# One plan for the order of all engines' instructions in the expert units

## The chip, the cores and the metric

The kernel runs on one core of a Trainium2 chip. The metric is device time in microseconds, the median of three runs; lower is better. Engines are named as in the profile: PE is TensorE (PEld its weight loads), DVE is VectorE, ACT is ScalarE, POOL is GpSimd, SP is SyncE, which here only issues DMAs.

## What is computed

Three stages follow one another: attention with pooled queries, a mixture of eight experts with one expert for each token, and a feed-forward block with g = h cos h. `w_in` and `w_out` of the last stage come as 64-bit floats.

```python
def _attn_ref(q, k, v):                      # (4, 8, 1152, 64)
    q_pool = q.reshape(B, H, S // 2, 2, D).mean(axis=3)
    scores = scale * np.matmul(q_pool, k.transpose(0, 1, 3, 2))
    attn = np.exp(scores - np.max(scores, axis=-1, keepdims=True))
    attn = attn / (np.sum(attn, axis=-1, keepdims=True) + 1e-09)
    return np.matmul(attn, v).astype(np.float32)

def _moe_ref(x, w_gate, w1, w2):             # 2304 tokens, 512 wide, 8 experts, 1024 hidden
    logits = x @ w_gate
    expert_idx = np.argmax(logits, axis=1)
    ...
    for e in range(E):
        mask = expert_idx == e
        h = np.maximum(x[mask] @ w1[e], 0.0)
        out[mask] = gate_w[mask, None] * (h @ w2[e])

def _moe2_ref(x, w_in, w_out):               # 512 -> 2048 -> 512
    h = x @ w_in
    g = h * np.cos(h)
    return (g @ w_out).astype(np.float32)
```

## The kernel before

**Stages.** Attention runs over 32 heads in an order that a `Plan` lays down (steps with times, sorted and traced in that order; `Plan.tie` then ties TensorE's instructions, and only those, to this order). Routing counts the tokens of each expert and writes each token's number to a slot table in HBM. The experts follow, then the cosine blocks of 512 tokens.

**Precision.** Each float32 operand is split into a high and a low part, so a product is three matmuls (high x high, high x low, low x high). Making a high part is a copy on ScalarE, a low part a subtraction on VectorE or GpSimd.

**Expert units.** The experts are sorted by size and handled in twelve units (`UNIT`, L473): ten of 256 tokens, the last two of 128. Units 0 to 2 belong to the first expert, 3 and 4 to the second, 5 and 6 to the third, 7 to 11 to one expert each. A unit (`Experts.unit`, L960) works through four chunks of the hidden width. For a full unit, `first` makes 24 matmuls into a `ph` bank (two banks), ScalarE makes `hh` with a Relu, VectorE `hl`; `second` makes 24 matmuls of 512 columns with `hh` and `hl` into two `py` banks. First products run two chunks ahead (`HP = 2`). A half unit has the tokens as stationary operand: `tokens_first`, a Relu copy `hs` on ScalarE, two transposes by TensorE (`turned`), then `hh`, `hl` and `second`. At a unit's end `py` is scaled by the gate to `ys`, the token's number is copied beside it, and ScalarE's queue stores it to `y_d`.

**Work around the units.** (1) Gathers: `Tokens` loads 128 slot numbers `ix` and fetches the token rows `xg` by an indirect DMA on GpSimd, TensorE transposes them, `xh` and `xl` are made (`split_transposed`, L1171), and one column of `xg`, the gate, is copied by VectorE (L1089). (2) Weights: a chunk's `w1` and `w2` are loaded by SP into one of three `raw` buffers, ScalarE makes the high half, VectorE or GpSimd (`PLOW`: chunk 3) the low half (`weight_steps`, L1119; `Pipe`, L1149). An expert has eight such halves; they go into the buffers of the expert two before it. (3) Narrowing (`Narrow.step`, L1208): 32 steps turn the 64-bit words of `w_in` and `w_out` into float32: a load on SP, five instructions on VectorE, two on ScalarE, one multiply on GpSimd (L1229), and a store. `NSTEP` (L509) says how many each unit gets. (4) The first cosine block's rows are gathered and transposed (`load_block`, L1092).

**What sets the order.** The framework traces all instructions in the order of the Python code and then schedules them, engine by engine, with a timeline of its own; an instruction runs in the queue of its engine in the order so found, and waits on semaphores. `issue_after(x)` ties a block's instructions behind `x` on `x`'s engine. In the experts, only such ties stand: weight loads, narrowing steps and gathers are traced between the chunks of a unit:

```python
            for k in range(NSTEP[u]):
                between[k * NCH // NSTEP[u]].append((1, step))
```

## Time and profile before

| | us |
|---|---|
| median of three runs (lowest to highest) | 1257.46 (1253.23 to 1261.61) |
| the profiled execution | 1258.61 |
| its span, from the first to the last instruction | 1257.0 |
| attention, up to unit 0's first matmul | 543.7 |
| unit 0 | 24.5 |
| units 1 to 11 | 270.1 |
| cosine blocks | 418.7 |

Over the span TensorE is busy 94%, VectorE 74%, ScalarE 58%, GpSimd 44%. The busy time of matmuls is modelled, and matmuls overlap; the pace is read from their starts. An engine handles its queue in order, so an instruction that waits holds all behind it. A bracket such as [5.23 <-DVE hl_u L987] gives the idle time of the engine before the instruction and what ended it. A row of a stretch gives its bounds, its length, the busy time and count of each engine's instructions, the granted clock of TensorE as a share of full speed, the mean busy share of the 16 DMA engines, and what they moved. In rows 2 the first stretch holds units 1 to 11; the others are units 1, 2, 3 to 7, 8, 9, 10 and 11.

### The profile page before, as it was taken

Reading aid. Unit: us, or ns where it says so; the run is one execution under the profiler, and the core shown is the slowest. Engines: PE = TensorE matmul, PEld = TensorE weight load, DVE = VectorE, ACT = ScalarE, POOL = GpSimd, SP = SyncE. Lnnn points to the kernel's source line nnn. Section 1 sums busy time; section 2 is a strip of 40 time slices with the busy share of each in tenths; the row PEclk is TensorE's granted clock in tenths of the full one; section 3 lists DMA queues with packets and bytes.
Section 4 is the critical chain, followed back from the end, with each engine's and each line's share of the span. In section 5 each row is a group of like instructions: output and inputs, shape, how many; then the busy total and the mean of one; then the engine's idle time right before and its main releaser. Section 6 shows DMA issues by size and latency. Waiting matters only on the chain. (4 is left out here: it accounts for less than half of the span.)

```text
span 1257.0 us, 26782 instructions
## 1 busy us (share of the span) xinstructions
...
## 2 busy tenths in 40 slices
...
GB/s 198 116 104 137 138 148 116 111 113 142 124 118 96 101 41 118 58 106 118 234 287 300 270 292 288 281 171 123 18 48 24 1 30 40 1 51 1 1 34 17
DMA packets 116729, 148.20 MB, mean 118 GB/s; under 512 B 32336, under 2 KB 73072, under 8 KB 116592
## 3 DMA queue, kind: packets, MB, share of 16 engines
...
q8 instruction: 82, 1.34, 0.5%
...
## 5 line engine op out<-in xcount | busy, mean ns | idle before, releaser
L324 POOL TENSOR_TENSOR pl<-pf,ph 128x576 f16<-128x576 f32 x186 | 240.2, 1297 | 92.6 <-ACT ph L320 46.6
L264 DVE TENSOR_REDUCE mm<-pm 128x1 f32<-128x384 f32 x432 | 226.1, 549 | 61.4 <-PE pm L254 52.3
L294 PE MATMUL pst<-q,k 128*128 128x288 f32 x576 | 175.8, 319 | 8.9 <-DVE pl L315 6.1
L1280 ACT ACTIVATE a<-a,hpi 128x512 f32<-128x512 f32 (+1 forms) x80 | 54.5, 681 | 199.2 <-DVE a L1279 199.2
L295 PE MATMUL pst<-q,k 66*128 66x288 f32 x576 | 165.5, 302 | 0.3 <-DMA q<-mx 0.2
L519 POOL DMA_INDIRECT out_dram<-os,token x16 | 16.3, 1022 | 325.2 <-PE po L1295 159.5
L344 PE MATMUL po<-va,ph 128*128 128x66 f16 (+1 forms) x1440 | 152.1, 195 | 0.9 <-DVE xs L368 0.6
L254 PE MATMUL pm<-k,q 128*128 128x384 f32 x384 | 142.5, 391 | 11.0 <-DVE mm L264 4.4
L346 PE MATMUL po<-va,pl 128*128 128x66 f16 (+1 forms) x1440 | 149.7, 195 | 2.5 <-POOL pl L324 1.3
L345 PE MATMUL po<-va,ph 128*128 128x64 f16 (+1 forms) x1440 | 150.2, 193 | 0.0
L344 PEld LDWEIGHTS <-ph 128*128 128x128 f16 (+1 forms) x1440 | 132.8, 101 | 18.1 <-issue 10.5
L346 PEld LDWEIGHTS <-pl 128*128 128x128 f16 (+1 forms) x1440 | 134.5, 100 | 3.4 <-POOL pl L324 1.8
L345 PEld LDWEIGHTS <-ph 128*128 128x128 f16 (+1 forms) x1440 | 134.5, 100 | 0.9 <-issue 0.6
L305 ACT ACTIVATE pf<-pst 128x576 f32<-128x576 f32 x186 | 122.5, 658 | 17.0 <-PE pst L295 12.5
L320 ACT CAST ph<-pf 128x576 f16<-128x576 f32 x186 | 127.7, 687 | 1.7
L294 PEld LDWEIGHTS pst<-q,k 128*128 128x128 f32 x576 | 111.3, 193 | 14.8 <-DVE pl L315 7.2
L1270 PE MATMUL ch<-zh,w1h_m 128*128 128x512 f32 (+1 forms) x320 | 120.0, 375 | 3.3 <-ACTq L1536 3.3
L1270 PE MATMUL ch<-zh,w1l_m 128*128 128x512 f32 (+1 forms) x320 | 119.7, 374 | 0.0
L1270 PE MATMUL ch<-zl,w1h_m 128*128 128x512 f32 (+1 forms) x320 | 119.6, 374 | 0.0
L1295 PE MATMUL po<-w2h_m,gh 128*128 128x512 f32 x288 | 114.7, 398 | 0.0
L1295 PE MATMUL po<-w2l_m,gh 128*128 128x512 f32 x288 | 114.2, 397 | 0.0
L295 PEld LDWEIGHTS pst<-q,k 66*128 66x128 f32 x576 | 111.2, 193 | 0.7 <-DMA q<-mx 0.4
...
## 6 DMA issues: line engine op xcount, KB each, us to landing
w1r_e<-in_moe_w_dram SPq DMA_DIRECT2D x32, 512.0 KB, 5.0
w2r_e<-in_moe_w_dram SPq DMA_DIRECT2D x32, 512.0 KB, 6.3
...
raw<-in_moe_w_in_dram SPq DMA_DIRECT2D x16, 512.0 KB, 5.4
```

Of the source, the lines that this page charges most:

```text
L254: nc.tensor.matmul(ps[:, o], self.st[i]["q1"][:, q0 : q0 + P], self.st[i]["k1"][:, ks], start=True, stop=True)
L264: self.nc.vector.tensor_reduce(mm[:, ci, g : g + 1], pm[:, :MK], axis=AX.X, op=ALU.max)
L294: nc.tensor.matmul(o, s["k1"][:, ks], s["q1"][:, q], start=True, stop=False)
L295: nc.tensor.matmul(o, self.k2[i % 3][: D + 2, ks], self.q2[i % 4][: D + 2, q], start=False, stop=True)
L305: nc.scalar.activation(s["pf", u], pst, AF.Exp, scale=0.0625)
L320: self.nc.scalar.copy(ph, pf)
L324: low = self.nc.gpsimd.tensor_sub(self.piece(s["pl"], u), s["pf", u], self.piece(s["ph"], u))
L344: nc.tensor.matmul(po[:, :66], hi, va[:, c, D:130], start=(c == 0), stop=False)
L345: nc.tensor.matmul(po[:, :D], hi, va[:, c, :D], start=False, stop=False)
L346: self.product = nc.tensor.matmul(po[:, :66], lo, va[:, c, D:130], start=False, stop=(c == NK - 1))
L1270: nc.tensor.matmul(ph[:, :n], wt[:, c, fs], z[:, c, :n], start=(k == 0), stop=(k == 3 * NDC - 1))
L1295: nc.tensor.matmul(po[j], g[:, ts], wt[:, f % FC, :], start=(f == 0 and k == 0), stop=(f == NFC2 - 1 and k == 2))
```

## The change

Unit 0 keeps its form, with three narrowing steps traced into it. From unit 1 to unit 11 every action is a step of one new `Plan`, `seq`, whose offsets from the unit's start stand in `E`, `UT` and `SMALL`; `seq.engines` has all five engines, so that `tie` fixes the order of the instructions of each of them. To this end the unit, the weight halves, the gathers, the first cosine block and the narrowing step are cut into single instructions or small groups (`Unit`, `weight_parts`, `turn_steps`, `Block`, `Narrow.parts`). A half unit's chunks are interleaved by `SMALL` (first product, transposes, second product). The gate copy stands behind `xl`, also for the two gathers made during attention (`Tokens.turn`). `NSTEP` gives units 1, 4 and 5 one step less each, unit 0 three (`NEARLY0`). The first cosine block is fetched and transposed from unit 10 on. In the routing, `first` is tied behind VectorE's latest row maximum (`behind`). `BEHIND` and `FLATE` are zero.

```diff
         self.span = start, end
         self.steps = []
-        self.last = None
+        self.last = {}
+        self.engines = (mybir.EngineType.PE,)
 
...
         order = mybir.DependencyInfo(mybir.DependencyClass.NoSync, mybir.DependencyReason.DATA)
         for i in made:
-            if i.engine == mybir.EngineType.PE:
-                if self.last is not None:
-                    self.tc.add_manual_dep(i, self.last.name, order)
-                self.last = i
+            if i.engine in self.engines:
+                if i.engine in self.last:
+                    self.tc.add_manual_dep(i, self.last[i.engine].name, order)
+                self.last[i.engine] = i
...
+HS = 2
+NEARLY0 = 3
+UT = (12.2, 22.5)
+E = dict(ix=1.62, f=2.81, sf=1.43, h=0.02, l=0.65, y=0.1, yn=3.0, g=1.0, gj=3.0, gt=8.17, sg=0.64,
+         sgt=5.0, r0=4.0, r1=12.5, g1=12.07, gt1=7.27, gj1=1.0, n1=8.0, sr=3.8, rs=2.8, rl=7.0,
+         rw=1.0, n0=2.0, nl=9.46, z0=0.04, z=3.8, zj=3.4, zt=4.5)
+SMALL = ((0.0, 2.9, 4.5), (1.43, 5.9, 7.7), (3.1, 7.5, 9.3), (6.1, 9.1, 10.7))
+TIED = ("PE", "Activation", "DVE", "Pool", "SP")
+BEHIND = 0
+FLATE = 0.0
 SSTEP = 2.5
...
-NSTEP = (0, 3, 2, 6, 4, 6, 3, 3, 3, 2, 0, 0)
+NSTEP = (0, 2, 2, 6, 3, 5, 3, 3, 3, 2, 0, 0)
...
+class Unit:
+
...
+    def first(self, c):
+        nc, w, x = self.nc, self.weights[c][0], self.tokens
+        ph = self.ph[c] = self.ex.ph.tile([P, FC, U], F32, tag="ph", name=f"ph_{self.name}_{c}")
+        for i in range(FC if self.n == U else 1):
             k = 0
             for d in range(NDC):
...
+                for wt, z in ((w[0], x.xh), (w[1], x.xh), (w[0], x.xl)):
+                    if self.n == U:
+                        o, a, b = ph[:, i, :], wt[:, d, i * P : (i + 1) * P], z[:, d, :]
+                    else:
+                        o, a, b = ph[:, 0, :], z[:, d, :P], wt[:, d, :]
+                    self.mm = nc.tensor.matmul(o, a, b, start=(k == 0), stop=(k == 3 * NDC - 1))
                     k += 1
...
+    def hide(self, c):
+        self.hs[c] = self.ex.p2.tile([P, FC * P], F32, tag="hs", name=f"hs_{self.name}_{c}", bufs=HS)
+        self.relu = self.nc.scalar.activation(self.hs[c], self.ph[c][:, 0, :], AF.Relu)
+
+    def turn(self, c):
+        self.ph[c] = self.ex.ph.tile([P, FC, U], F32, tag="ph", name=f"phT_{self.name}_{c}")
+        for i in range(FC):
+            at = slice(i * P, (i + 1) * P)
+            self.nc.tensor.transpose(self.ph[c][:, 0, at], self.hs[c][:, at], self.ex.ident)
+
+    def high(self, c):
+        p2, bufs = self.ex.p2, self.ex.ahead + 1
+        hh, hl = (p2.tile([P, FC, U], F32R, tag=t, name=f"{t}_{self.name}_{c}", bufs=bufs) for t in ("hh", "hl"))
+        self.h[c] = hh, hl
+        if self.n == U:
+            self.relu = self.nc.scalar.activation(hh, self.ph[c], AF.Relu)
+        else:
+            self.relu = self.nc.scalar.copy(hh[:, 0, :], self.ph[c][:, 0, :])
+
+    def lower(self, c):
+        hh, hl = self.h[c]
+        if self.n == U:
+            self.low = self.nc.vector.scalar_tensor_tensor(
+                hl, self.ph[c], 0.0, hh.bitcast(F32), op0=ALU.max, op1=ALU.subtract
+            )
+        else:
+            self.low = self.nc.vector.tensor_sub(hl[:, 0, :], self.ph[c][:, 0, :], hh[:, 0, :].bitcast(F32))
+
+    def second(self, c):
...
+    def number(self, j):
+        ys = self.ys[j] = self.ex.p2.tile([P, XR], F32, tag="ys", name=f"ys_{self.name}_{j}")
+        self.nc.vector.tensor_copy(ys[:, DM:], self.tokens.ix[:, j : j + 1].bitcast(F32).to_broadcast([P, IW]))
+
+    def scale(self, j):
+        self.nc.scalar.activation(
+            self.ys[j][:, :DM], self.py[j], AF.Copy, scale=self.tokens.gate[:, j : j + 1]
+        )
+
...
+    def steps(self, j, ps, tag):
+        cols, gate = slice(j * P, (j + 1) * P), self.gate[:, j : j + 1]
+        return turn_steps(self.nc, ps, tag, self.ident, self.xg[j], self.xh, self.xl, cols, f"{self.name}_{j}") + [
+            lambda: self.nc.vector.tensor_copy(gate, self.xg[j][:, DM : DM + 1])
+        ]
...
+        with self.tc.issue_after(getattr(low, "ins", low)):
+            self.nc.vector.tensor_copy(self.gate[:, j : j + 1], xg[:, DM : DM + 1])
...
+def weight_parts(nc, to, rp, w1, w2, c, name, pool, out, k):
...
+    def issue():
+        w[0] = rp.tile([P, n, f], F32, tag="raw", name=f"{tag}r_{name}")
+        nc.sync.dma_start(w[0], src)
+
+    def high():
+        if isinstance(to, list):
+            out[k] = to[k]
+        else:
+            pool_c = to(c) if callable(to) else to
+            out[k] = tuple(
+                pool_c.tile([P, n, f], F32R, tag=f"{tag}{h}{c % NCH}", name=f"{tag}{h}_{name}") for h in "hl"
+            )
+        nc.scalar.copy(out[k][0], w[0])
+
+    def lower():
+        (nc.gpsimd if pool[k] else nc.vector).tensor_sub(out[k][1], w[0], out[k][0].bitcast(F32))
+
+    return issue, high, lower
...
+def turn_steps(nc, ps, tag, ident, src, hi, lo, cols, name):
+
+    w = {}
+
+    def turn():
+        w[0] = ps.tile([P, NDC * P], F32, tag=tag, name=f"pt_{name}")
+        for c in range(NDC):
+            nc.tensor.transpose(w[0][:, c * P : (c + 1) * P], src[:, c * P : (c + 1) * P], ident)
+        w[0] = w[0].rearrange("p (c t) -> p c t", t=P)
+
+    def high():
+        nc.scalar.copy(hi[:, :, cols], w[0])
+
+    def lower():
+        return nc.vector.tensor_sub(lo[:, :, cols], w[0], hi[:, :, cols].bitcast(F32))
+
+    return [turn, high, lower]
...
+        def load():
+            w["raw"] = p.tile(shape + [2], I32, name="raw64")
+            nc.sync.dma_start(w["raw"], src)
+            w["lo"], w["hi"] = w["raw"][:, :, 0].bitcast(U32), w["raw"][:, :, 1]
+
+        def word():
+            v = w["v"] = self.ps.tile(shape, I32, name="v64")
+            nc.vector.tensor_scalar(v, w["hi"], 3, 0x3FFFFFFF, op0=ALU.logical_shift_left, op1=ALU.bitwise_and)
+
+        def sign():
+            v = w["v"]
+            nc.vector.scalar_tensor_tensor(v, w["hi"], -0x40000000, v, op0=ALU.bitwise_and, op1=ALU.bitwise_or)
+
+        def square():
+            w["t"] = p.tile(shape, I32, name="t64")
+            nc.scalar.activation(w["t"].bitcast(F32), w["hi"].bitcast(F32), AF.Square)
+
+        def keep():
+            v = w["v"].bitcast(F32)
+            nc.vector.scalar_tensor_tensor(
+                v, w["t"].bitcast(F32), 3.4332275390625e-05**2, v, op0=ALU.is_ge, op1=ALU.mult
+            )
+
+        def rest():
+            w["l"] = p.tile(shape, F32, name="l64")
+            nc.scalar.activation(w["l"], w["lo"], AF.Copy, scale=2.0**-52)
+
+        def power():
+            nc.vector.tensor_single_scalar(w["t"], w["v"], -0x800000, op=ALU.bitwise_and)
+
+        def scale():
+            nc.gpsimd.tensor_mul(w["l"], w["l"], w["t"].bitcast(F32))
+
+        def total():
+            o = p.tile(shape, F32, name="o64")
+            nc.vector.tensor_add(o, w["v"].bitcast(F32), w["l"])
+            self.store()
+            self.made = (dst, o)
+
+        return [load, word, sign, square, keep, rest, power, scale, total]
...
+        def behind(f):
+            with tc.issue_after(att.reduced):
+                f()
...
+        for k in range(NEARLY0):
+            between[k * NCH // NEARLY0].append((1, step))
+        xs.append(unit_slots(AHEAD))
+        with tc.issue_after(product):
+            ex.unit("u0", ws[0], xs[0], YROW[0], between)
+        seq = Plan(tc, -math.inf, math.inf)
+        seq.engines = tuple(getattr(mybir.EngineType, e) for e in TIED)
+        zp = []
+        start = [0.0, 0.0]
+        for _, _, n in UNIT[1:]:
+            start.append(start[-1] + UT[n == U])
+        narrow_at = []
         for u, (i, j, n) in enumerate(UNIT):
             if u == 0:
...
+                continue
+            t, big = start[u], n == U
+            if u + AHEAD < NU:
+                seq(t + E["ix"], lambda u=u: xs.append(unit_slots(u + AHEAD)))
+
+            def unit(u=u, i=i):
+                units[u] = Unit(ex, f"u{u}", ws[i], xs[u], YROW[u])
+
+            def do(f, u=u):
+                return lambda *args: getattr(units[u], f)(*args)
+
+            seq(t, unit)
+            for c in range(NCH):
+                if big:
+                    z = t + E["f"] * (c if c < HP + 1 else 2 * c - HP)
+                    seq(z, do("first"), c)
+                    seq(z + E["f"] + E["h"], do("high"), c)
+                    seq(z + E["f"] + E["h"] + E["l"], do("lower"), c)
+                    c2 = min(c, 1) * 2 + HP + 1 + max(c - 1, 0)
+                    seq(t + E["f"] * c2, do("second"), c)
+                else:
+                    z = t + SMALL[c][0]
+                    seq(z, do("first"), c)
+                    seq(z + E["sf"] + E["h"], do("hide"), c)
+                    z = t + SMALL[c][1]
+                    seq(z, do("turn"), c)
+                    seq(z + 0.3 + E["h"], do("high"), c)
+                    seq(z + 0.3 + E["h"] + E["l"], do("lower"), c)
+                    seq(t + SMALL[c][2], do("second"), c)
+            for j2 in range(n // P):
+                z = t + UT[big] + E["y"] + 0.7 * j2
+                seq(z, do("scale"), j2)
+                seq(z - E["y"] - E["yn"], do("number"), j2)
+                seq(z + 0.1, do("store"), j2)
+            if u + 1 < NU:
+                for j2 in range(UNIT[u + 1][2] // P):
+                    z = t + (E["g1"] + E["gj1"] * j2 if u == 1 else (E["g"] if big else E["sg"]) + E["gj"] * j2)
+
+                    def turn(k, u=u, j2=j2, w={}):
+                        if k == 0:
+                            w[0] = xs[u + 1].steps(j2, ex.px, "pt")
+                        w[0][k]()
+
+                    seq(z, lambda u=u, j2=j2: xs[u + 1].fetch(j2))
+                    z += E["gt1"] if u == 1 else E["gt"] if big else E["sgt"]
+                    for k, d in enumerate((0.0, 0.8, 1.5, 1.6)):
+                        seq(z + d, turn, k)
+            raws = []
+            r0 = t + (E["r0"] if big else E["sr"])
+            if u == 1:
+                r0 = t + E["r1"]
+                raws = [(1, c, k) for c in range(NCH) for k in range(2)]
+            elif u == 2:
+                r0 = start[1] + E["r1"] + 8 * E["rs"]
+                raws = [(2, c, k) for c in range(NCH) for k in range(2)]
+            elif j == UNITS[i] - 1 and i + 2 < NE:
+                raws = [(i + 2, c, k) for c, k in ((0, 0), (1, 0), (2, 0), (0, 1), (3, 0), (1, 1), (2, 1), (3, 1))]
+            elif u >= NU - 2:
+                raws = [(NE, c, k) for c in range(2 * (u - NU + 2), 2 * (u - NU + 2) + 2) for k in range(2)]
+            for r, (e, c, k) in enumerate(raws):
+                z = r0 + E["rs"] * r
+
+                def raw(part, e=e, c=c, k=k, w={}):
+                    if (e, c) not in made:
+                        if e < NE and e not in number:
+                            number[e] = entry(rt.ordered, e, NE - 1)
+                        while len(ws[e]) <= c:
+                            ws[e].append([None, None])
+                        made[e, c] = weight_parts_of(e, c, ws[e][c])
+                    made[e, c][k][part]()
+
+                seq(z - E["rl"], raw, 0)
+                seq(z, raw, 1)
+                seq(z + E["rw"], raw, 2)
             for k in range(NSTEP[u]):
-                between[k * NCH // NSTEP[u]].append((1, step))
+                narrow_at.append(t + (E["n1"] + k * (UT[1] + E["n0"] - E["n1"]) / NSTEP[u] if u == 1 else E["n0"] + k * UT[big] / NSTEP[u]))
             if u == ZU - 1:
...
+                def close():
+                    narrow.store()
+                    ns.close()
+                    zp.append(ctx.enter_context(tc.tile_pool(name="zp0", bufs=1, side="right", reuse_waits="tile")))
+
+                seq(t + E["z0"], close)
+            if u == ZU - 1:
+                blk = Block(nc, xq, "xg", ex.px, "pt", ident, y_d[: YROW[NZ], :], rt.source, token, *blocks[0])
+                seq(t + E["z"], lambda: blk.open(zp[0]))
+                for k in range(blk.nt):
+                    seq(t + E["z"] + E["zj"] * k, blk.fetch, k)
+
+                    def turn(p, k=k, w={}):
+                        if p == 0:
+                            w[0] = blk.steps(k)
+                        w[0][p]()
+
+                    for p, d in enumerate((0.0, 0.8, 1.5, 1.6)):
+                        seq(t + E["z"] + E["zj"] * k + E["zt"] + d, turn, p)
+        todo = narrow.todo
+        narrow.todo = []
+        for z, job in zip(narrow_at, todo):
+            w = narrow.parts(*job)
+            for f, d in zip(w, (-E["nl"], 0.0, 0.65, 0.0, 1.5, 0.7, 2.2, 3.0, 4.6)):
+                seq(z + d, f)
+        assert len(narrow_at) == len(todo) or not todo
+        seq.run()
```

## Rows read from the trace of the kernel before

**Rows 1.** The page: the span.

```profile
span 1257.0 us, 26782 instructions
```

**Rows 2.** Stretches: length; busy PE, PEld, DVE, ACT, POOL; clock, DMA share, GB/s.

```profile
568.20:838.30 270.10, 248.00 (x1545) 220.96 (x1544) 208.28 (x330) 148.64 (x221) 113.83 (x82) 0.97 0.77 252
568.20:600.00 31.80, 26.57 (x153) 23.97 (x152) 15.06 (x42) 10.38 (x17) 9.67 (x9) 0.89 0.38 113
600.00:626.30 26.30, 24.52 (x162) 22.02 (x160) 19.63 (x30) 13.33 (x20) 8.25 (x7) 1.00 0.67 228
626.30:750.30 124.00, 118.87 (x768) 106.46 (x766) 109.51 (x175) 73.45 (x111) 62.71 (x44) 1.00 0.88 286
750.30:780.00 29.70, 25.61 (x144) 22.91 (x143) 24.89 (x34) 17.41 (x25) 13.66 (x10) 0.89 0.86 285
780.00:804.00 24.00, 22.87 (x150) 20.52 (x149) 19.88 (x29) 14.03 (x19) 12.48 (x10) 1.00 0.85 286
804.00:826.00 22.00, 18.17 (x110) 15.67 (x109) 12.99 (x18) 13.13 (x22) 7.05 (x5) 0.92 0.76 241
826.00:838.30 12.30, 11.39 (x69) 9.39 (x68) 6.34 (x9) 6.91 (x12) 0.00 (x0) 1.00 0.57 187
```

**Rows 3.** The same of L980 alone (PE, PEld): one first product.

```profile
609.73:612.56 2.83, 2.83 (x24) 2.79 (x23) 1.00 0.36 101
```

**Rows 4.** The same of L1019 alone: 12 matmuls of the second product.

```profile
688.42:691.19 2.77, 2.77 (x12) 2.08 (x12) 1.00 0.66 216
```

**Rows 5.** The same of L1175 alone: one tile's transposes.

```profile
607.68:608.03 0.35, 0.35 (x4) 0.35 (x4) 1.00 0.77 109
```

**Rows 6.** Timeline of PE: start, duration, instruction, [idle before it, releaser].

```profile
580.67 0.58 PE L980 MATMUL ph_u<-xh_u,w1h_e 128*128 128x256 f32 x1 [5.23 <-DVE hl_u L987]
...
758.99 0.50 PE L1019 MATMUL py_u<-w2h_e,hh_u 128*128 128x512 f32 x1 [2.75 <-ACT hh_u L986]
761.53 0.58 PE L980 MATMUL ph_u<-xh_e,w1h_e 128*128 128x256 f32 x1 [1.34 <-DVE hl_u L987]
...
809.89 0.44 PE L1008 MATMUL phT_u<-ident,hs_u 128*128 128x128 f32 x2 [1.58 <-ACT hs_u L1002]
813.56 0.51 PE L1019 MATMUL py_u<-w2h_e,hh_u 128*128 128x512 f32 x1 [1.73 <-ACT hh_u L1010]
```

**Rows 7.** Three more stretches, columns as in rows 2.

```profile
543.67:571.20 27.53, 27.31 (x197) 25.11 (x195) 20.79 (x107) 5.71 (x10) 13.12 (x10) 1.00 0.55 179
580.67:585.90 5.23, 5.23 (x24) 5.23 (x25) 0.55 (x1) 0.00 (x0) 0.00 (x0) 0.50 0.00 0
640.00:660.00 20.00, 17.86 (x113) 15.77 (x113) 17.50 (x28) 11.48 (x19) 7.87 (x7) 1.00 0.96 326
```

**Rows 8.** Timeline of DVE in units 1, 2 and 4.

```profile
578.23 0.15 DVE L1089 COPY gate_e<-xg_e 128x1 f32<-128x1 f32 x1 [7.04 <-DMA xg_e<-x_d,ix_e]
...
579.94 0.68 DVE L987 SCALAR_TENSOR_TENSOR hl_u<-ph_u,hh_u 128x512 fp32r<-128x512 f32 x1
...
615.48 1.22 DVE L1142 TENSOR_TENSOR w2l_e<-w2r_e,w2h_e 128x1024 fp32r<-128x1024 f32 x1
...
620.51 2.34 DVE L1142 TENSOR_TENSOR w2l_e<-w2r_e,w2h_e 128x1024 fp32r<-128x1024 f32 x1 [0.21 <-ACT w2h_e L1141]
...
664.94 0.68 DVE L1230 TENSOR_TENSOR o<-v,l 128x512 f32<-128x512 f32 x1
665.54 0.68 DVE L1228 TENSOR_SCALAR t<-v 128x512 int32<-128x512 int32 x1
```

**Rows 9.** DMA issues, 543 to 838: count, KB, us to landing.

```profile
w2r_e<-in_moe_w_dram SPq DMA_DIRECT2D x29, 512.0 KB, 6.4
xg_e<-x_d,ix_e POOLq DMA_INDIRECT x18, 5.6
yg<-y_d,source POOLq DMA_INDIRECT x4, 6.7
```

**Rows 10.** Timeline of POOL in unit 2.

```profile
620.48 1.29 POOL L1229 TENSOR_TENSOR l<-l,t 128x512 f32<-128x512 f32 x1 [10.99 <-ACT w2h_e L1141]
```

298 lines of the change are left out of this document (120 added, 178 removed).

## The prediction

> **What bounds the kernel now.** The page comes first: the program is one span of 1257.0 us [rows 1]; the profiled execution took 1258.61 us, so 1.6 us lie around the span. It is 1.15 us above the median of the three runs (1257.46) and inside their range, so the sum below starts from 1258.61. Next I read the busy time by stretches, cut at the edges of the twelve expert units as TensorE's timeline shows them (units overlap by a few matmuls, so an edge is good to about 1 us). Units 1 to 11, the only part that gets the new plan, last 270.1 us [rows 2]. TensorE is busy in 248.0 of them, so it idles 22.1 us, and its mean granted clock is 0.97, which at two levels (full and half) means that some 0.03 x 270.1 = 8 us more went to half-speed matmuls. The reader is to see that the loss is not even: unit 1 takes 31.8 us, unit 8 takes 29.7 and unit 10 takes 22.0, all three at a mean clock of 0.89 to 0.92, while units 3 to 7 take 124.0 us, 24.8 each.
>
> What a unit must take comes from gap-free stretches: 24 matmuls of the first product take 2.83 us [rows 3], 12 of the second 2.77 us [rows 4], and the four transposes of one gathered tile 0.35 us [rows 5]. A full unit is four of each product and two tiles for the next unit: 4 x 2.83 + 4 x 2.77 + 2 x 0.35 = 23.1 us. For a half unit I take what unit 11 took, 12.3 us with 0.9 idle [rows 2]. So TensorE is the bound at 23.1 us a unit, and what stands above it is waiting.
>
> Then TensorE's timeline, for what the waits are [rows 6]: 5.23 us in unit 1 until VectorE's `hl`; 2.75 and 1.34 us in unit 8 until `hh` and `hl`; 1.58 and 1.73 us in unit 10 until `hs` and `hh`. In unit 1 VectorE's timeline names what was in front: a copy of a gate column, 0.15 us long, sat 7.04 us until the gathered rows had landed, and the `hl` that TensorE needed came behind it at 579.94 [rows 8]. That stall is paid twice: behind the 5.23 us of idling the next 24 matmuls ran at a granted clock of 0.50, the lower level of 1.2 GHz, and took 5.23 us instead of 2.83 [rows 7]. Unit 8's mean clock of 0.89 tells of the same, 0.11 x 29.7 = 3.3 us [rows 2].
>
> Two other resources are near: VectorE is busy 109.5 of 124.0 us in units 3 to 7 and the DMA engines 0.88 of it at 286 GB/s [rows 2]. The densest 20 us ran at 326 GB/s with a share of 0.96 [rows 7]; 286 x 124.0 = 35.5 MB at 326 GB/s is 109 us, 21.8 a unit. Both have room down to TensorE's 23.1, but little.
>
> **The change part by part.** No arithmetic is removed; of units 1 to 11 every instruction keeps its size. What changes is the order on five queues, three of 32 narrowing steps that move to unit 0, and the place of the gate copies.
>
> *Gate copies behind `xl`.* The copy can no longer stand in front of `hl` while a gather is under way. That removes unit 1's 5.23 us and the 5.23 - 2.83 = 2.4 us at half clock: 7.6 us. Late next is the gather itself: the wait moves to TensorE's transposes, planned 7.27 us behind the fetch in unit 1 and 8.17 in the others; a gather lands after 5.6 us [rows 9] and its issue queues a little, so I price it at nothing there, and at 1.5 us a unit if POOL is late.
>
> *Three narrowing steps in unit 0.* A step is five VectorE instructions at 0.60 us from start to start [rows 8], 3.0 us. VectorE was busy 20.8 of 27.5 us from the start of unit 0 to the end of the routing at 571.2 [rows 7], so 6.7 us were free. If the 9.0 us go into those gaps, the queue ends 2.3 us later, at 573.5; if all come behind the routing, at 580. Unit 1's third first product needs `hl` of chunk 0 and could start where TensorE stopped, at 580.67 - 5.23 = 575.4 [rows 6]. So 0 to 4.8 us of stall come back, and up to 2.4 more at half clock. The loads of these steps can be issued early, which speaks for the gaps; I take 2, and 0.5 for the ends. **Unit 1: 31.8 to 23.1 + 2.5 = 25.6, gain 6.2.** The bounds are 1.5 and 8.7.
>
> *Half units.* The old code puts chunk c's transposes straight behind the first product of c+1, where they wait for `hs`, and the second product straight behind the transposes, where it waits for `hh`. The new offsets put another product into each of these places. Unit 10 then costs 12.3 + 0.35 for unit 11's tile + 0.7 for two tiles of the first cosine block. New there: these transposes are planned 4.5 us behind their fetch, but such a fetch lands after 6.7 us [rows 9]. TensorE, in fixed order, waits 2.2 us once; the later tiles have the same delay and cost nothing more. **Unit 10: 22.0 to 15.5, gain 6.5** (bounds 4 and 8.7). **Unit 11: 12.3 to 13.0, loss 0.7**, for the other two tiles.
>
> *Full units 2 to 9 under the plan.* What is queued behind a late load is the risk: ScalarE's weight cast waits for it, with `hh` behind; VectorE's first narrowing instruction too, with `hl` behind. The plan issues a weight load 7.0 us before its cast, a load lands after 6.4 us [rows 9], and with three `raw` buffers it cannot issue before the subtraction three halves back ends. One round is 6.4 + cast and subtraction at about 1.22 each [rows 8] = 8.84 us for three halves, 2.95 a half where the plan has 2.8; eight halves take 23.6 us. So units that load an expert cannot go far below 23.6 plus what collides. I take 24.2 for units 3 to 7, **gain 124.0 - 121.0 = 3.0**; for unit 2 24.3, **gain 2.0**; for unit 8, whose two stalls and half clock go, 24.4, **gain 5.3**; for unit 9 23.2, **gain 0.8**. Bounds of the four together: 19.5 if all reach 23.1 (unit 9: 22.7), 0 if the loads keep today's pace.
>
> *Unit 3* carries six narrowing steps: 6 x 3.0 + six `hl` and `xl` at 0.60 + two weight subtractions at 1.22 + copies of 0.5 = 24.5 us of VectorE, above 23.1; that is in the 24.2 mean.
>
> *The rest at nothing.* The second `first` of the routing and four gate copies in the attention move behind work of VectorE that is traced before them; attention's end is set by TensorE, and I leave 1 us either way. The cosine blocks are not touched; their first weights are loaded in units 10 and 11 as before.
>
> Sum: 6.2 + 2.0 + 3.0 + 5.3 + 0.8 + 6.5 - 0.7 = 23.1. **1258.6 - 23.1 = 1235.5, forecast 1235 us.**
>
> **The rivals.** *A, the load ring sets the pace.* Denser units mean fuller DMA engines. If a load takes 1 us more, a round is 9.84 us, 3.28 a half, 26.2 us for eight; six units (2, 4, 6 to 9) carry such loads, 2.0 us each more than I took, 12 us: 1247. For it: the share of 0.96 at 326 GB/s [rows 7]. Against it: 21.8 us a unit is enough for the bytes.
>
> *B, VectorE and GpSimd hold each other up.* A subtraction that takes 1.22 us took 2.34 us when a GpSimd narrowing multiply of 1.29 us started 0.03 us before it [rows 8, 10]. A fixed order can repeat such a meeting in each unit. A unit with three narrowing steps and eight halves gives VectorE 9.0 + 4.2 + 6 x 1.22 = 20.5 us; five GpSimd instructions that each hold one subtraction for 1.12 add 5.6: 26.1 us. Units 4, 6, 7 and 8 then take 1.8 more than I took: 1242. The Trainium skill (SBUF — State Buffer, section Who interferes with whom) says that a VectorE instruction with two SBUF inputs contends with a GpSimd one that reads SBUF, and that the one issued second waits it out. By that rule the row is no accident; the trace agrees in size.
>
> *C, slower.* One order for five engines couples them: where one load is late by more than the two `ph` banks can hide, ScalarE, VectorE and TensorE all stop since none can take other work first. If that happens once a unit, each looks like unit 8, which lost 4.1 us idle and 3.3 us to half clock and took 29.7 us [rows 2, 6]. Nine units at 29.7 with 15.5 and 13.0 are 295.8, 25.7 over today: 1284. It decides from (270.1 - 28.5) / 9 = 26.8 us a unit up. Most likely place: SP, where a narrowing load that waits for one of two `raw64` buffers holds the weight loads behind it. Against it: in the median a load lands within the planned lead, 6.4 against 7.0 us [rows 9].
>
> **How the numbers follow.** Forecast 0.55, B 0.12, A 0.18, C 0.15. A measurement of this kernel can tell about 1% from no change, 12.6 us: below 1246 counts as faster, which holds the forecast and B, 0.67; A lies at the edge within 1%, 0.18; C 0.15. The best end is every unit at its floor with only the late fetch left: 8.7 + 19.5 + 6.5 - 0.7 = 34, 1224. The range from 1224 to 1260 holds the forecast, B and A and leaves out C and little more.
>
> **What would show it.** Right: no gate copy with a wait of microseconds; units 1 to 9 near 24 us and no stretch at half clock among them; unit 10 near 15 with one wait on the fetched rows; VectorE near 0.9 busy. Wrong: TensorE waiting 2 us or more for `hh` or `hl` in every unit (C); ScalarE's casts waiting on weight loads with a steady 3.3 us from cast to cast (A); subtractions over 2 us beside GpSimd's (B); a stop of 3 us at the start of unit 1 with the three early steps in front of `hl`.

## The result, and the profile after

The kernel after takes 1246.24 us in the median of six executions (1240.16 to 1265.53) against 1258.44 (1253.23 to 1263.64) for six of the kernel before; the ratio is 0.9887, with a 95% interval of 0.9859 to 0.9916. A second measurement of the same kernel (below) gave 0.9936 (0.9896 to 0.9976). The ratio leaves out the execution of 1265.53 us, which ran at a lower granted clock (0.971) than the others. So the change saves some 8 to 14 us, about 1%, where 23 were forecast: faster, as said, and by between a third and three fifths as much.

The profiled execution of after took 1240.16 us. The page says:

```profile
span 1238.6 us, 26710 instructions
```

That is 18.4 us less than the span of before [rows 1]. Not all of it belongs to the change: attention ended 2.4 us earlier (541.3 against 543.7), in a stage whose end moves by more than that between executions (last section). The cosine blocks took 418.0 us against 418.7. What is left, 15.3 us, is the expert units. The following rows are after's stretches, with the columns of rows 2 and in the same order (units 1 to 11; then unit 1, 2, 3 to 7, 8, 9, 10, 11); the last one is unit 4 alone.

```profile
565.83:820.59 254.76, 241.29 (x1545) 217.41 (x1544) 207.95 (x355) 148.47 (x218) 116.70 (x80) 0.99 0.84 271
565.83:593.13 27.30, 23.65 (x153) 21.14 (x151) 27.06 (x76) 11.55 (x18) 9.78 (x7) 1.00 0.70 214
593.13:617.11 23.98, 23.61 (x153) 21.38 (x153) 17.85 (x28) 15.30 (x21) 14.24 (x9) 1.00 0.88 282
617.11:739.55 122.44, 118.36 (x762) 107.48 (x760) 106.76 (x169) 72.28 (x107) 59.40 (x40) 0.99 0.87 284
739.55:764.88 25.33, 23.78 (x153) 21.18 (x152) 20.69 (x32) 15.60 (x23) 12.84 (x8) 1.00 0.89 302
764.88:788.81 23.93, 23.06 (x150) 20.82 (x149) 18.37 (x27) 15.11 (x21) 12.16 (x8) 1.00 0.85 279
788.81:807.50 18.69, 15.74 (x93) 13.50 (x92) 8.72 (x16) 9.88 (x18) 6.94 (x6) 0.91 0.79 251
807.50:820.59 13.09, 13.09 (x91) 11.92 (x90) 8.50 (x13) 8.76 (x16) 1.35 (x3) 1.00 0.69 202
640.39:668.01 27.62, 24.86 (x154) 22.60 (x153) 24.88 (x41) 16.65 (x24) 12.14 (x9) 0.94 0.89 305
```

Units 1 to 11 take 254.8 us against 270.1 [rows 2], a gain of 15.3. TensorE's idle time there falls from 22.1 to 13.5 us, and the mean granted clock rises from 0.97 to 0.99. Three units still stand out: unit 1 at 27.3, unit 4 at 27.6 and unit 10 at 18.7. TensorE's timeline has one or two stops in each (start, duration, instruction, idle time before it and what ended it):

```profile
574.64 0.39 PE L1024 MATMUL ph_u<-xh_u,w1h_e 128*128 128x256 f32 x1 [2.98 <-DVE hl_u L1049]
...
649.00 0.58 PE L1024 MATMUL ph_u<-xh_e,w1h_e 128*128 128x256 f32 x1 [2.77 <-DVE hl_u L1049]
...
792.47 0.44 PE L1035 MATMUL phT_u<-ident,hs_u 128*128 128x128 f32 x2 [0.67 <-ACT hs_u L1029]
798.40 0.38 PE L1024 MATMUL ph_u<-w1h_e,xh_e 128*128 128x256 f32 x1 [1.95 <-ACT hs_u L1029]
```

The stop for `hl` in unit 1 falls from 5.23 to 2.98 us, and the waits of 2.75 and 1.34 us in unit 8 [rows 6] to 0.87 and 0.68, both for `hl`. VectorE's waits for gathered rows in front of a gate copy are gone. In their place VectorE waits for GpSimd. Two lines of VectorE's waits in the experts of before (instruction, what it waited for, us in total, times, longest), then the line of after:

```profile
DVE gate_e L1089 <- DMA xg_e<-x_d,ix_e: 12.6, 6, 7.0
...
DVE o L1230 <- POOL l L1229: 4.8, 4, 1.6
```

```profile
DVE o L1345 <- POOL l L1341: 16.6, 19, 2.6
```

`o` is the last of the five VectorE instructions of a narrowing step; it needs the multiply `l` that GpSimd makes after VectorE's fourth (L1338). The plan puts VectorE's fourth and fifth 2.4 us apart, and 19 times that was too little.

### The profile page after: what moved, and what is told of

Its sections match the earlier page's. It is cut to its first block, busy times and chain, and to the rows that moved or that the text cites. A ratio compares the mean times of both kernels' runs of the same rounds, so it can differ in the third digit from the quotient of the medians.

```text
span 1238.6 us, 26710 instructions
## 1 busy us (share of the span) xinstructions
PE 1177.7 (95%) x10271; PEld 1027.0 (83%) x10271; DVE 934.7 (75%) x1990; ACT 733.3 (59%) x1274; POOL 554.8 (45%) x529
## 3 DMA queue, kind: packets, MB, share of 16 engines
q8 instruction: 82, 1.34, 0.5%
## 5 line engine op out<-in xcount | busy, mean ns | idle before, releaser
L1397 ACT ACTIVATE a<-a,hpi 128x512 f32<-128x512 f32 (+1 forms) x80 | 54.5, 682 | 204.4 <-DVE a L1396 194.5
L531 POOL DMA_INDIRECT out_dram<-os,token x16 | 16.3, 1019 | 323.4 <-PE po L1412 157.9
L306 ACT ACTIVATE pf<-pst 128x576 f32<-128x576 f32 x186 | 122.5, 659 | 17.5 <-PE pst L296 13.0
```

The costliest lines, as they stand in the source:

```text
L306: nc.scalar.activation(s["pf", u], pst, AF.Exp, scale=0.0625)
```

## The experiments

Executions differ by more than some effects here, so each kernel is read by stages of its profile too. The table is worked out from TensorE's timeline: the end of attention (start of the first expert matmul) and the lengths of groups of units in us. In some kernels unit 0 and unit 1 overlap, so they stand together. Each row is one profiled execution. The two of after differ by up to 2.5 us in a group of units and by 2.9 in all twelve, so smaller differences are not read from one row alone; the ratios come from all executions.

| kernel | attention ends | units 0, 1 | 2, 3 | 4 | 5 to 9 | 10, 11 | units 0 to 11 | ratio to before (95%) |
|---|---|---|---|---|---|---|---|---|
| before | 543.7 | 56.4 | 50.7 | 24.0 | 127.3 | 36.2 | 294.7 | |
| after | 541.3 | 51.9 | 47.3 | 27.6 | 120.8 | 31.8 | 279.3 | 0.9887 (0.9859 to 0.9916) |
| after, second measurement | 548.6 | 54.4 | 47.1 | 27.2 | 123.0 | 30.4 | 282.2 | 0.9936 (0.9896 to 0.9976) |
| before, gate copies late | 546.8 | 48.1 | 48.6 | 23.5 | 131.6 | 33.5 | 285.3 | 0.9933 (0.9898 to 0.9968) |
| after, TensorE alone tied | 549.0 | 55.5 | 64.0 | 23.2 | 129.0 | 35.0 | 306.7 | 1.0111 (1.0064 to 1.0158) |
| after, no steps in unit 0 | 543.4 | 48.6 | 48.8 | 27.9 | 124.8 | 34.0 | 284.2 | 0.9938 (0.9908 to 0.9969) |
| after, four steps in unit 3 | 544.5 | 54.5 | 48.2 | 27.3 | 122.2 | 35.1 | 287.2 | 0.9954 (0.9919 to 0.9989) |
| after, three buffers `raw64` | 548.2 | 52.8 | 47.2 | 27.4 | 120.8 | 31.6 | 279.8 | 0.9953 (0.9919 to 0.9987) |
| after, sum later | 550.9 | 51.7 | 47.7 | 29.4 | 117.3 | 31.8 | 277.9 | 0.9954 (0.9918 to 0.9990) |
| after, casts later | 545.6 | 54.7 | 47.1 | 27.8 | 121.8 | 31.8 | 283.2 | 0.9958 (0.9921 to 0.9994) |
| after, old half units | 542.2 | 52.8 | 47.8 | 26.7 | 122.3 | 36.2 | 285.7 | 0.9959 (0.9929 to 0.9990) |
| both causes away | 547.0 | 54.9 | 47.5 | 23.2 | 125.7 | 31.3 | 282.5 | 0.9912 (0.9876 to 0.9948) |
| candidate 1 | 544.1 | 49.5 | 48.9 | 25.1 | 122.5 | 33.0 | 278.9 | 0.9912 (0.9884 to 0.9940) |
| candidate 2 | 548.9 | 49.0 | 48.2 | 23.2 | 125.5 | 34.9 | 280.8 | 0.9896 (0.9866 to 0.9926) |

### After, a second time

> The kernel after, unchanged, looked at a second time, to tell what of its stage times belongs to the kernel. If the stops belong to the plan, they come again at the same places: unit 1 at 27 to 30 us with a stop of about 3 us for hl, unit 4 at 27 to 28 us with a stop of 2 to 3 us, unit 10 at 18 to 22 us with a stop for hs. If they are chance meetings, they sit in other units. The end of attention, which came 2.4 us earlier in the first look, is expected anywhere between 541 and 547 us. Ratio 0.987 to 0.994.

Stretches of the second profile: units 1 to 11, unit 1, unit 4, unit 10.

```profile
573.13:830.75 257.62, 243.47 (x1545) 218.66 (x1544) 208.33 (x355) 148.67 (x218) 114.83 (x80) 0.98 0.81 268
573.13:603.02 29.89, 26.43 (x154) 23.78 (x152) 27.20 (x78) 11.56 (x18) 9.63 (x7) 0.89 0.65 207
650.09:677.33 27.24, 25.03 (x154) 22.72 (x152) 23.85 (x38) 16.43 (x24) 11.86 (x8) 0.94 0.89 298
800.32:817.67 17.35, 14.47 (x94) 11.96 (x92) 8.60 (x13) 10.09 (x18) 5.94 (x6) 1.00 0.79 258
```

The stops come again in units 1 (2.79 us), 4 (2.21) and 10 (1.62), for the same tiles, so they belong to the plan. Unit 9 stops for 2.00 us, where the first profile has 0.87. Attention ended at 548.6, 7.3 us later than in the first profile. Units 1 to 11 came to 257.6 us, so the gain there is 12.5 to 15.3 us.

### Gate copies late, nothing else

```diff
--- before
         xg = self.xg[j]
-        split_transposed(
+        low = split_transposed(
...
-        self.nc.vector.tensor_copy(self.gate[:, j : j + 1], xg[:, DM : DM + 1])
+        with self.tc.issue_after(getattr(low, "ins", low)):
+            self.nc.vector.tensor_copy(self.gate[:, j : j + 1], xg[:, DM : DM + 1])
```

> The kernel before with one part of the change alone: the gate copies are tied behind xl on VectorE. The recorded reasoning: the 7.04 us that a gate copy sat in front of hl in unit 1 go, with the half clock behind them, so unit 1 falls from 31.8 to about 24.3 us, nothing else moves, and the ratio to before is 0.994 (7.6 of 1258 us). Rival: another wait takes the place of the removed one (VectorE reaches hl late behind the routing and the narrowing anyway), unit 1 stays above 28 us, and the ratio is 0.997 or more.

Units 0 and 1 of before, then of this kernel, then its unit 5:

```profile
543.67:600.04 56.37, 50.92 (x328) 46.29 (x325) 32.93 (x128) 14.75 (x25) 21.78 (x17) 0.94 0.44 138
```

```profile
546.76:594.85 48.09, 48.06 (x327) 43.78 (x325) 32.76 (x126) 14.55 (x25) 19.79 (x15) 1.00 0.53 162
...
666.92:697.85 30.93, 25.20 (x155) 22.49 (x154) 29.04 (x44) 16.21 (x25) 11.39 (x9) 0.89 0.83 280
```

Units 0 and 1 fall by 8.3 us (7.6 expected), TensorE is busy in all but 0.03 of their 48.09 us, and the ratio is 0.9933 (0.994 expected). "Nothing else moves" was wrong, though: unit 8's two waits shrink to 1.65 and 0.93 us, unit 5 has stops of 2.18 and 3.56 us, and unit 6 waits 2.54 us for gathered rows. In the framework's order one small edit moves the stops of units far behind it. By the stages this part alone brings 9.4 of the 12.5 to 15.4 us that units 0 to 11 gain in the whole change, 8.3 of them in units 0 and 1; by the ratios it cannot be told from the whole.

### The order of TensorE alone

```diff
--- after
-TIED = ("PE", "Activation", "DVE", "Pool", "SP")
+TIED = ("PE",)
```

> The kernel after, with only TensorE tied to the plan; the other four engines' instructions are again ordered by the framework. Theory: the fixed order of all engines is what brings units 2 to 9 to 24 us; without it units 3 to 7 go back from 122.4 to about 124 us and unit 8 from 25.3 to about 29, so the whole is some 5 to 8 us slower than after: ratio to before 0.993 to 0.996. Rival: the gain comes from TensorE's order, the late gate copies and the interleaved half units, and the other queues' order is worth nothing: ratio to before 0.987 to 0.990, as after. Second rival: the single-step narrowing in an order chosen by the framework puts more in front of hl, and it is slower than before.

It is slower than before by 1.1%, the second rival. Unit 3 as a stretch, and from TensorE's timeline its stop:

```profile
635.89:668.50 32.61, 26.17 (x153) 23.86 (x152) 28.71 (x46) 17.94 (x27) 16.96 (x11) 0.84 0.91 308
```

```profile
648.17 0.58 PE L1024 MATMUL ph_u<-xh_e,w1h_e 128*128 128x256 f32 x1 [6.44 <-DVE hl_u L1049]
```

Units 1 to 3 take 30.9, 31.4 and 32.6 us, each with a stop of 2.95 to 6.44 us for `hl`, at mean clocks of 0.89, 0.89 and 0.84. Cut into single steps and left to the framework, VectorE's queue has narrowing and weight subtractions in front of `hl`, and ScalarE's has weight casts and `ys` in front of `hh`: in unit 3 the first `hh` began at 644.84 and its `hl` at 647.45, though the unit had started at 635.89. TensorE, in fixed order, can take nothing else first. The order of the other four engines is worth 24.5 to 27.4 us beside TensorE's (306.7 against 282.2 and 279.3); but 12.0 of that (306.7 against 294.7) only repair what cutting up and tying TensorE alone would cost. Two of these costs have nothing to do with the narrowing: with the plan's order go the places of the number copies, which waited 16.3 us for stores on VectorE here, and of the gate copies, 12.8 us.

### No narrowing steps in unit 0

```diff
--- after
-NEARLY0 = 3
+NEARLY0 = 0
...
-NSTEP = (0, 2, 2, 6, 3, 5, 3, 3, 3, 2, 0, 0)
+NSTEP = (0, 2, 3, 6, 3, 6, 3, 3, 3, 3, 0, 0)
...
-            between[k * NCH // NEARLY0].append((1, step))
+            between[k * NCH // max(NEARLY0, 1)].append((1, step))
```

> The kernel after without the three early narrowing steps in unit 0; units 2, 5 and 9 get one more each. Theory: 9 us of VectorE work in unit 0 push the routing and hl of unit 1 back; without them unit 1's stop of 2.98 us goes and the unit falls from 27.3 to about 24.3 us, units 2, 5 and 9 gain at most 0.5 each: ratio to before about 0.987. Rival: the routing alone makes hl late; the stop in unit 1 stays at 2 us or more and the ratio at 0.989 or above.

Unit 1:

```profile
567.97:592.05 24.08, 23.41 (x153) 21.07 (x151) 17.76 (x45) 10.54 (x17) 7.40 (x7) 1.00 0.46 148
```

VectorE's busy time in unit 1 falls from 27.06 to 17.76 us and the unit from 27.3 (29.9) to 24.08, as expected: the three early steps cost 3.2 to 5.8 us there. But the whole is no faster. Units 2, 5 and 9 got the three steps, and the unit behind each of them grew. Unit 3 takes 24.95 us (23.28 and 23.25 in the two profiles of after), unit 6 25.76 (23.78, 23.80), unit 10 20.97 (18.69, 17.35). In unit 10 the reason stands in ScalarE's queue: of two stores of narrowed words the second waits for VectorE's `o`, with `ys` and `hs` behind it, and TensorE stops for `hs` for 4.62 us.

```profile
792.49 5.02 ACTq L1356 DMA_DIRECT2D wo_d<-o  x2
797.55 0.69 ACT L1073 ACTIVATE ys_u<-py_u,gate_e 128x512 f32<-128x512 f32 x1 [4.04 <-DVE o L1345]
```

The other two kernels with a third step in unit 9 (four steps in unit 3, candidate 2) stop there for 4.64 and 5.86 us, and units 10 and 11 take 34.0 to 35.1 us in all three; in the seven profiles with two steps there, all engines tied and the new order of the half units, they take 30.4 to 33.0.

### What holds unit 4

Four runs. First, fewer steps in unit 3:

```diff
--- after
-NSTEP = (0, 2, 2, 6, 3, 5, 3, 3, 3, 2, 0, 0)
+NSTEP = (0, 2, 2, 4, 3, 6, 3, 3, 3, 3, 0, 0)
```

> The kernel after with four narrowing steps in unit 3 instead of six; units 5 and 9 get one more each. Theory: six steps overload VectorE in unit 3, its backlog makes the first hl of unit 4 late by 2.77 us, and the half clock behind that costs about 1.6 more. Then unit 4 falls from 27.6 to about 23.8 us, units 5 and 9 gain at most 0.5 each, and the ratio to before goes from 0.9887 to about 0.986. Rival: the stop in unit 4 comes from one collision of VectorE with GpSimd or from a late load, not from the count of steps; unit 4 stays above 26.5 and the ratio at 0.989.

My theory failed: unit 4 takes 27.26 us, with a stop of 2.24. The traces show why. In after, VectorE's timeline at the start of unit 4 (640.39) is a solid row of narrowing; `hh` of chunk 0 was there from 646.3, and its `hl` came 2 us later, behind them:

```profile
646.82 0.70 DVE L1321 SCALAR_TENSOR_TENSOR v<-raw,v 128x512 int32<-128x512 int32 x1
647.66 0.69 DVE L1345 TENSOR_TENSOR o<-v,l 128x512 f32<-128x512 f32 x1
648.26 0.68 DVE L1049 SCALAR_TENSOR_TENSOR hl_u<-ph_u,hh_u 128x512 fp32r<-128x512 f32 x1
```

With four steps in unit 3 VectorE is not full (busy 17.15 of 24.37 us in that unit), but it stands still for GpSimd's multiply, twice for 1.50 us, with the number copy and `hl` behind it in its queue (unit 4 starts at 647.20):

```profile
647.57 0.69 DVE L1345 TENSOR_TENSOR o<-v,l 128x512 f32<-128x512 f32 x1 [1.50 <-POOL l L1341]
...
648.77 0.16 DVE L1070 COPY ys_u<-ix_e 128x16 f32<-128x16 f32 x1
...
652.62 0.69 DVE L1345 TENSOR_TENSOR o<-v,l 128x512 f32<-128x512 f32 x1 [1.50 <-POOL l L1341]
...
654.54 0.68 DVE L1049 SCALAR_TENSOR_TENSOR hl_u<-ph_u,hh_u 128x512 fp32r<-128x512 f32 x1
```

ScalarE closes the ring: its store of `ys` waits for the number copy, and behind the store stand the second `ys` and `hh`:

```profile
649.01 0.33 ACTq L1079 DMA_DIRECT2D y_d<-ys_u  x1
...
652.29 0.58 ACT L1042 ACTIVATE hh_u<-ph_u 128x512 fp32r<-128x512 f32 x1
```

`ys` was done at 647.41; the store went at 649.01, and `hh` at 652.29. So there are two causes, and each is enough by itself. The next run takes away the second alone:

```diff
--- after
-            for f, d in zip(w, (-E["nl"], 0.0, 0.65, 0.0, 1.5, 0.7, 2.2, 3.0, 4.6)):
+            for f, d in zip(w, (-E["nl"], 0.0, 0.65, 0.0, 1.5, 0.7, 2.2, 3.0, 7.0)):
```

> The kernel after with the last VectorE instruction of each narrowing step planned 7.0 instead of 4.6 us behind the first. Theory: in the fixed order VectorE waits for GpSimd's multiply about 19 times, 16 to 19 us in all, with hl queued behind; with 2.4 us more between them the waits fall below 5 us, unit 4 falls from 27.6 to about 25 us and units 6 to 9 by 0.5 us each: 4 to 5 us in all, ratio about 0.985. Rival: VectorE is late for another reason (late narrowing loads), the time saved there is waited for elsewhere, and units 2 to 9 take the same 195.7 us within 1.5.

VectorE's waits for GpSimd fall as expected:

```profile
DVE o L1345 <- POOL l L1341: 5.3, 5, 1.2
```

Units 5 to 9 gain more than was said (3.5 us against the first profile of after, where units 6 to 9 were to gain 0.5 each); unit 4 does not; it takes 29.4 us. These rows are units 5 to 9 of after (123.0 us in its second profile) and of this kernel:

```profile
668.01:788.81 120.80, 117.07 (x758) 105.63 (x757) 98.96 (x153) 72.57 (x104) 60.32 (x40) 1.00 0.87 284
```

```profile
679.67:797.00 117.33, 116.43 (x758) 105.68 (x756) 103.33 (x152) 72.73 (x103) 62.37 (x39) 1.00 0.87 292
```

117.33 us are 23.5 a unit, with 0.9 us of idling in five units. Unit 8, which has three steps in every kernel, says the same over all profiles: with all engines tied it takes 25.1 to 26.1 us in the seven with the sum at 4.6 and 23.2 to 24.4 in the four with 7.0. The whole kernel isn't measurably faster (0.9954, where 0.985 was expected), with attention ending at 550.9 in the profiled execution.

Third, a third buffer for the 64-bit words, in case late narrowing loads were behind it:

```diff
--- after
-            w["raw"] = p.tile(shape + [2], I32, name="raw64")
+            w["raw"] = p.tile(shape + [2], I32, name="raw64", bufs=3)
```

> The kernel after with three buffers instead of two for the 64-bit words of the narrowing steps. Theory: six steps in 22.5 us leave 7.5 us for two, while a load lands after about 6.3 us and needs some 3 us more until its buffer is free; SyncE waits for the buffer with the weight loads of the fourth unit queued behind it. With a third buffer the loads come in time, unit 4 falls from 27.6 to about 24.5 us, and SyncE's wait for a narrowing buffer falls from 50 to below 15 us. Rival: the DMA engines, busy 0.84 of the time, set the pace; the loads take longer instead, unit 4 stays above 26.5 us, and the ratio stays near 0.989.

SyncE's wait for that buffer falls from 46.8 to 33.9 us only, and unit 4 stays at 27.35 us. A third buffer is no cure, and the next run brings unit 4 down with two; so the buffers are not the cause.

Fourth, both causes away, with two suspects of unit 10 beside them (there, casts and transposes come later):

```diff
--- after
-         sgt=5.0, r0=4.0, r1=12.5, g1=12.07, gt1=7.27, gj1=1.0, n1=8.0, sr=3.8, rs=2.8, rl=7.0,
-         rw=1.0, n0=2.0, nl=9.46, z0=0.04, z=3.8, zj=3.4, zt=4.5)
+         sgt=5.0, r0=4.0, r1=12.5, g1=12.07, gt1=7.27, gj1=1.0, n1=8.0, sr=6.0, rs=2.8, rl=7.0,
+         rw=1.0, n0=2.0, nl=9.46, z0=0.04, z=3.8, zj=3.8, zt=5.9)
...
-NSTEP = (0, 2, 2, 6, 3, 5, 3, 3, 3, 2, 0, 0)
+NSTEP = (0, 2, 3, 4, 3, 6, 3, 3, 3, 2, 0, 0)
...
-            for f, d in zip(w, (-E["nl"], 0.0, 0.65, 0.0, 1.5, 0.7, 2.2, 3.0, 4.6)):
+            for f, d in zip(w, (-E["nl"], 0.0, 0.65, 0.0, 1.5, 0.7, 2.2, 3.0, 7.0)):
```

> The kernel after with two causes taken away together in each of two places. For unit 4: four narrowing steps in unit 3 (one more each in units 2, 5 and 6) and the last VectorE instruction of a step 7.0 us behind the first. For unit 10: weight casts of units 10 and 11 2.2 us later, and the first cosine block's rows transposed 5.9 instead of 4.5 us behind their fetch, 3.8 us apart. Theory: in unit 4 the stop had two causes, each enough by itself (VectorE's backlog from six steps; with four steps its waits for GpSimd's multiply), so that taking one away (27.3 and 29.4 us) showed nothing; with both gone unit 4 takes 23.5 to 24.5 us. In unit 10 a late w_in cast held hs, and with that gone the late fetched rows held TensorE; with both gone the unit takes 15.5 to 16.5 us. Units 5 to 9 stay at 23.2 to 24. Unit 1 keeps its 27 to 30. Whole: 6 to 7 us below after, ratio about 0.987 to 0.989. Rival: the burst of DMA traffic at the start of unit 4 (three weight loads, two stores, a gather) holds ScalarE's first casts and with them hh; unit 4 stays above 26.5.

The two steps taken from unit 3 went to units 2 and 5; unit 6 keeps its three, other than the expectation says. Units 4, 7, 10 and 11:

```profile
649.37:672.60 23.23, 23.23 (x154) 21.20 (x152) 22.54 (x37) 15.39 (x22) 10.37 (x9) 1.00 0.94 316
...
721.73:750.98 29.25, 25.29 (x153) 22.49 (x152) 25.24 (x38) 17.67 (x24) 16.22 (x10) 0.94 0.91 305
798.26:813.89 15.63, 13.28 (x89) 11.82 (x88) 7.58 (x14) 8.64 (x16) 7.39 (x7) 1.00 0.77 261
813.89:829.52 15.63, 14.06 (x94) 12.29 (x93) 9.32 (x14) 9.06 (x17) 2.99 (x5) 1.00 0.63 194
```

Unit 4 takes 23.23 us and TensorE is busy in all of it: the two causes are shown together (a DMA share of 0.94 at 316 GB/s didn't hold it, so the rival falls). The two candidates below agree: with four steps in unit 3 and the later sum unit 4 takes 23.22 us again, with five 25.1. Unit 10 takes 15.6, but not because its causes are gone: TensorE still waits 2.35 us for `hs`, now behind the store of unit 9's last step, which waits for the later sum and stands in front of `ys`; and a cosine tile's transposes went to unit 11, which goes from 13.1 to 15.6. So the pair gains nothing, and unit 7 takes 29.25 with a wait of 2.70 us for gathered rows. The sum of all units is 282.5, as in the second profile of after.

### Casts later, and the old order in the half units

```diff
--- after
-         sgt=5.0, r0=4.0, r1=12.5, g1=12.07, gt1=7.27, gj1=1.0, n1=8.0, sr=3.8, rs=2.8, rl=7.0,
+         sgt=5.0, r0=4.0, r1=12.5, g1=12.07, gt1=7.27, gj1=1.0, n1=8.0, sr=6.0, rs=2.8, rl=7.0,
```

> The kernel after with the four weight casts of units 10 and 11 planned 2.2 us later (sr 6.0 instead of 3.8, with their loads). Theory: in unit 10 ScalarE waits for the first w_in load, which lands 7.6 us after its issue, with hs behind it; put later, the cast no longer holds hs, the stop of 2 us or more and the half clock behind it go, and unit 10 falls from 18.7 (22.0 and 21.0 in the two runs before this one) to about 16 us. Rival: the load itself is held by the ring of three raw buffers and comes later by as much, so the stop only moves to another chunk and unit 10 stays at 18.5 or more; or the last casts push into the cosine blocks, which then start later.

Unit 10 stays at 18.33 us. The waits for `hs` fall from 0.67 and 1.95 to 0.49 us in all, but a tile of the cosine block is late now:

```profile
814.91 0.66 PE L1256 MATMUL pt_y<-ident,yg 128*128 128x128 f32 x4 [2.65 <-DMA yg<-y_d,source]
```

That is the late fetch that the prediction had priced at 2.2 us. In after the stop for `hs` comes first, and TensorE waits for these rows 0.82 us at most.

```diff
--- after
-SMALL = ((0.0, 2.9, 4.5), (1.43, 5.9, 7.7), (3.1, 7.5, 9.3), (6.1, 9.1, 10.7))
+SMALL = ((0.0, 2.86, 3.9), (1.43, 6.0, 7.0), (4.6, 9.1, 10.1), (7.7, 10.8, 11.8))
```

> The kernel after with the two half units in the order of the kernel before: the transposes of a chunk stand right behind the first product of the next, and the second product right behind them; all other steps as after. The recorded reasoning gave the interleaved order 6.5 us in unit 10 and -0.7 in unit 11. Theory: with the old order TensorE waits again for hs and hh in each chunk, units 10 and 11 together go from 31 to 32 us (18.7 and 13.1) to 34 to 36, and half clock comes back. Rival: what sets these two units is the arrival of weights and rows, and the order of products is worth less than 1 us.

Units 10 and 11:

```profile
791.72:811.69 19.97, 14.98 (x94) 12.13 (x92) 9.93 (x17) 9.84 (x17) 7.50 (x8) 1.00 0.80 262
811.69:827.92 16.23, 14.02 (x89) 11.68 (x88) 8.58 (x13) 8.74 (x16) 0.87 (x3) 1.00 0.53 165
```

36.2 us together, as long as in before, against 31.8 and 30.4 in after: the interleaved order is worth 4.4 to 5.8 us. TensorE waited 2.01 us for `hh` in unit 10 and 1.52 in unit 11 here.

### Two candidates

Candidate 1 changes the offsets `sr`, `zj`, `zt` and the sum's 7.0 as the run with both causes away, and beside these:

```diff
--- after
-NEARLY0 = 3
+NEARLY0 = 1
...
-NSTEP = (0, 2, 2, 6, 3, 5, 3, 3, 3, 2, 0, 0)
+NSTEP = (0, 3, 3, 5, 3, 6, 3, 3, 3, 2, 0, 0)
```

Candidate 2:

```diff
--- after
-NEARLY0 = 3
+NEARLY0 = 1
...
-         sgt=5.0, r0=4.0, r1=12.5, g1=12.07, gt1=7.27, gj1=1.0, n1=8.0, sr=3.8, rs=2.8, rl=7.0,
-         rw=1.0, n0=2.0, nl=9.46, z0=0.04, z=3.8, zj=3.4, zt=4.5)
+         sgt=5.0, r0=4.0, r1=12.5, g1=12.07, gt1=7.27, gj1=1.0, n1=8.0, sr=5.0, rs=2.8, rl=7.0,
+         rw=1.0, n0=2.0, nl=9.46, z0=0.04, z=3.8, zj=3.8, zt=5.9)
...
-NSTEP = (0, 2, 2, 6, 3, 5, 3, 3, 3, 2, 0, 0)
+NSTEP = (0, 3, 3, 4, 3, 5, 4, 3, 3, 3, 0, 0)
...
-        for z, job in zip(narrow_at, todo):
+        for n, (z, job) in enumerate(zip(narrow_at, todo)):
...
-            for f, d in zip(w, (-E["nl"], 0.0, 0.65, 0.0, 1.5, 0.7, 2.2, 3.0, 4.6)):
+            for f, d in zip(w, (-E["nl"], 0.0, 0.65, 0.0, 1.5, 0.7, 2.2, 3.0, 7.0 if n < len(todo) - 1 else 4.6)):
```

> The kernel after with one early narrowing step in unit 0 instead of three, three steps in units 1 and 2, five in unit 3, six in unit 5, and the later sum, casts and transposes of the run before. A kernel meant to be faster than both. Theory: unit 1 falls from 27 to 30 us to 24 to 25, unit 4 to 24 to 25.5, units 5 to 9 stay at 23.2 to 24, unit 10 takes about 16: units 1 to 11 take about 247 us against 254.8 to 258.6, ratio to before 0.984 to 0.987. Rival: one early step is enough to push hl of unit 1 behind the routing, and three steps in unit 1 hold its second half: unit 1 stays above 27 and the ratio above 0.989.

> A second kernel meant to be faster than both: one early narrowing step in unit 0, three in units 1 and 2, four in unit 3, five in unit 5 as after (six there had made units 6 and 7 slower), four in unit 6, three in units 4 and 7 to 9; the last VectorE instruction of a step 7.0 us behind the first; weight casts of units 10 and 11 1.2 us later; the first cosine block's rows transposed 5.9 us behind their fetch. Theory: where VectorE's work of a unit stays below the unit's length and no wait for GpSimd stands in front of hl, a full unit takes its 23.2 to 24 us; so units 0 and 1 together take 49 to 50 us (51.9 and 54.4 in the two looks at after), units 2 to 9 189 to 192 us (195.7 to 198.5), units 10 and 11 31 to 32 us, and the ratio to before is 0.983 to 0.987. Rival: VectorE's work is too close to the length of the units everywhere, a step taken from one unit is missed in the next (unit 6 and 7 here), units 2 to 9 stay above 194 us, and the ratio is 0.989 or more.

Both are faster than before, neither is measurably faster than after (0.9912 and 0.9896). Candidate 2 shows why. Its units 4, 7, 8 and 10 as stretches, and TensorE's longest stops in 7 and 10:

```profile
646.12:669.34 23.22, 23.22 (x153) 21.20 (x152) 21.41 (x33) 15.03 (x22) 11.12 (x8) 1.00 0.88 299
...
717.44:748.28 30.84, 25.46 (x154) 22.32 (x152) 28.74 (x39) 16.84 (x24) 16.32 (x11) 0.94 0.88 289
748.28:771.52 23.24, 23.24 (x154) 21.20 (x153) 18.89 (x28) 15.29 (x22) 11.61 (x7) 1.00 0.87 291
...
794.88:815.45 20.57, 14.71 (x89) 13.08 (x88) 9.74 (x18) 9.69 (x17) 7.66 (x8) 0.83 0.72 231
```

```profile
737.95 0.66 PE L1256 MATMUL pt_e<-ident,xg_e 128*128 128x128 f32 x4 [3.44 <-DMA xg_e<-x_d,ix_e]
...
803.70 0.69 PE L1035 MATMUL phT_u<-ident,hs_u 128*128 128x128 f32 x2 [5.86 <-ACT hs_u L1029]
```

Units 4, 5 (23.23) and 8 sit at TensorE's floor (the prediction's 23.1 us), and what they gain is paid in units 7 and 10. In unit 7, behind the four narrowing steps of unit 6, VectorE is busy 28.74 of 30.84 us, and the second fetch of rows was issued 10.8 us into the unit, where the plan has 4.0, behind GpSimd's multiplies and a weight subtraction of 2.44 us. In unit 10 the second of two stores of narrowed words waited for VectorE's `o` and held `ys`, before which ScalarE idled 3.04 us, and `hs` behind it. The offsets can be moved, and each move so far opened another place. Whether some set of offsets holds all units at 23.2 us is open.

## Why the prediction was right, and where it was too large

The direction held, and so did the mechanism of the largest gains: a gate copy no longer stops `hl`, unit 8's waits shrink, and the half units' new order pays. The size did not hold. 1246 us lies inside 1224 to 1260, at the edge between "faster" and "within 1%", next to the price of rival A (1247), whose mechanism is not seen: that nearness is chance, and the total alone could not have told the forecast from A. The stages can. The sum of 23.1 us was 7.8 too high for units 1 to 11 in the first profile (15.3) and 10.6 in the second (12.5). In the first, unit 10 took 3.2 us more than forecast, unit 1 1.7, units 3 to 7 1.4, unit 8 0.9, unit 9 0.7. Of the signs for being right the first came, no gate copy with a wait of microseconds; but VectorE was busy 0.82 of units 1 to 11 where near 0.9 was said, and units 4 and 10 ran in part at half clock (means of 0.94 and 0.91). By its steps:

- **Gate copies.** 7.6 us; 8.3 measured by themselves. Right, in place, size and cause. "Late next is the gather, at nothing" held too.
- **Early narrowing steps.** Priced at 2 us of stall out of bounds from 0 to 4.8 and 2.4 at half clock. Without them unit 1 takes 24.08, so they cost 3.2 and 5.8 us, near the bad end. The mis-sized term is the room on VectorE: the prediction counted 6.7 free us in unit 0, before the routing was done, but the steps shared the queue with the routing and came in front of `hl` in unit 1, where VectorE was busy 27.06 of 27.30 us. Their stores, in ScalarE's queue, held `hh` too: it began at 570.89, after two stores that waited for VectorE, and `hl` at 573.91. Unit 1: 25.6 forecast, 27.3 and 29.9 measured. The prediction's own sign for this, a stop of 3 us at the start of unit 1 with the three early steps in front of `hl`, came true.
- **Unit 3's VectorE load.** The prediction worked out 24.5 us of VectorE work against 23.1 and put it into a mean. That step failed. Unit 3 itself takes 23.28; the backlog arrives in unit 4, whose first `hl` comes late, and the stop is paid twice, the second time at a lower clock (a mean of 0.62 and 0.68 in the 4 us behind it): 27.6 and 27.2 us where 24.2 was taken. Units 3 to 7 gain 1.6 instead of 3.0.
- **Full units 2 to 9.** Forecast 193 us (24.3, 121.0, 24.4, 23.2), measured 195.7 and 197.3. The two stalls of unit 8 shrank, as said, and its half clock went. What keeps units 7 to 9 above 23.2 is not the ring of weight buffers but a round trip that the prediction had not priced: VectorE's fourth narrowing instruction, GpSimd's multiply, VectorE's fifth, in two fixed queues. With the fifth later and the ring as it was, units 5 to 9 came to 23.5 each.
- **Half units.** 6.5 - 0.7 = 5.8; undoing the new order costs 4.4 to 5.8, so that term was right in size. Unit 11 took 13.1, as said. But unit 10 takes 18.7 and 17.4 instead of 15.5, for another reason than the late rows, and one that the prediction left out: ScalarE's cast waits for the first `w_in` load, which landed 7.6 us after its issue in both profiles where the plan allows 7.0, with `hs` behind it. With that cast later, the wait for `hs` fell and the late rows came forward, 2.65 us for a price of 2.2.
- **Rival A** (three buffers set the pace) is not seen: weight loads landed after 4.8 and 6.3 us in the median against 6.4 [rows 9], and units that load an expert ran at 23.2 us (unit 4 with both causes away, unit 8 of candidate 2). A fourth buffer was not tried.
- **Rival B** in its stated form fell. Of 50 weight subtractions recorded in the expert units of after one took over 1.6 us, against 8 of 48 in before: a fixed order did not repeat the meeting to VectorE's cost. GpSimd paid instead; 12 of its 32 multiplies took over 1.6 us (6 of 32 in before). These rows of after are one such meeting, on DVE and on POOL:

```profile
650.19 1.22 DVE L1222 TENSOR_TENSOR w1l_e<-w1r_e,w1h_e 128x1024 fp32r<-128x1024 f32 x1
```

```profile
650.45 2.10 POOL L1341 TENSOR_TENSOR l<-l,t 128x512 f32<-128x512 f32 x1 [0.46 <-DVE t L1338]
```

  The subtraction began 0.26 us earlier and kept its 1.22 us; the multiply took 2.10 instead of 1.29. In before the multiply began first and the subtraction took 2.34 [rows 8, 10]. The Trainium skill (SBUF — State Buffer, section Who interferes with whom) says that the order of issue decides which of the two waits; both traces agree.
- **Rival C** (a stop in every unit) did not come, but its mechanism did, in three units of eleven: one late instruction in a fixed queue, with `hl` or `hs` behind it, and half clock after that. The prediction gave it to all units or to none; a price for "in three units, at 3 us each" was missing, and that is about the 8 us that the sum was too high.

Gate copies and half units together make 12.7 to 14.1 us, and the early steps take 3.2 to 5.8 of it back; what the plan does in the other units is what lacks to the 12.5 to 15.3 measured, some 2 to 8 us; no run shows that part by itself.
